# Attention followed by a SwiGLU block: value products one pair later, the first sequence's exponentials summed on the tensor engine, weights rounded by integer operations

## The chip, the cores and the metric

The kernel runs on one NeuronCore of one Trainium2 chip. The metric is the device time of one execution in microseconds (us); the number given for a kernel is the median of several runs.

The engines of the core have queues of their own, each worked off in order: TensorE (PE in the profile, with its weight loads as PEld) does matmuls and transposes, VectorE (DVE), ScalarE (ACT) and GpSimd (POOL) work on tiles, and SyncE (SP) issues DMAs here. They meet at semaphores.

## The reference

Attention with normalised queries and keys, then a feed-forward block over its output, all in float32 (the weights arrive as float64):

```python
batch, n_heads, seq, head_dim = (8, 12, 448, 64)
n_tokens, d_model, d_ff = (3584, 768, 1536)

def rmsnorm(x, g):
    rms = np.sqrt(np.mean(x * x, axis=-1, keepdims=True) + 1e-06)
    return x / rms * g
q_n, k_n = (rmsnorm(q, g_q), rmsnorm(k, g_k))
scores = scale * np.matmul(q_n, k_n.transpose(0, 1, 3, 2))
attn = np.exp(scores - np.max(scores, axis=-1, keepdims=True))
attn = attn / (np.sum(attn, axis=-1, keepdims=True) + 1e-09)
x = np.matmul(attn, v)          # then (B,H,S,D) -> (B*S, H*D)

xn = x / rms(x) * rms_g
g = xn @ w_gate
silu = g * (1.0 / (1.0 + np.exp(-g)))
out = (silu * (xn @ w_val)) @ w_out
```

## The kernel before

There are 8 sequences of 448 tokens, and in each 12 heads that are worked two at a time: 6 pairs a sequence, 48 pairs in all (`g` counts them). `safe_scores` is the part that runs; a second version, `any_scores`, stands behind a flag that is not set for these inputs.

**A pair of heads.** `load_pair` issues five DMAs on SP. `norm_pair` squares q and k on ScalarE (L463), sums rows on VectorE (L466), and on GpSimd scales the sums, raises them to the power -1/2 (L469) and multiplies q by the result (L471). `turn_pair` transposes q and k on TensorE (L485) and copies them to SBUF, the query by ScalarE (L488) and the key by VectorE (L490). `score` does four score matmuls (two blocks of 112 keys by two heads, L500), ScalarE's exponentials (L504), and GpSimd's additions (L508 and L512) that sum the exponentials of the four key blocks into one tile `es` for each head: six additions a pair. It is called twice a pair. `values` does the value products (L520) and multiplies `es` by a matrix of ones (L524), which gives the softmax denominators; `divide` takes their reciprocal on VectorE (L532), multiplies (L537), and sums the squares of the result on ScalarE and GpSimd (L542, L543).

**The feed-forward.** When six pairs of a sequence are done, `rms_x` and `norm_x` normalise their output. `ffn_items` lists 24 projections of six matmuls (`gate` and `val`, L575) and six to eight output projections of 12 matmuls (L600). `fill`, which is called four times a pair, emits such items of the sequence before between the attention steps of the present one, by their cost in columns. So the first sequence's attention runs with no feed-forward beside it, and the last sequence's feed-forward runs alone. The projections write to two PSUM banks (`ps_f`), which VectorE empties (L584 and L590, behind ScalarE's tanh, L582).

**Weights.** `convert` turns a block of 128 x 768 float64 weights into float32 by its two 32-bit words: ScalarE's absolute value of the high word (L413), GpSimd's clip (L414), VectorE's shift and sign (L416, L417), then the power of two of the value (L420), the low word times that power (L422), and GpSimd's float addition (L423). There are 36 blocks: 12 of the gate, 12 of the value projection, which are also stored to DRAM for the later sequences, and 12 of the output projection. Three gate and three value blocks are converted during the first sequence's attention; the other 30 when the first sequence's feed-forward runs, each three projections ahead of its use. The float64 blocks come into two buffers (`raw_pool`).

**What sets the order.** The program lists the work pair by pair; a scheduler then orders each engine's instructions, so an engine's row of instructions can differ from the listing. A buffer's next use waits for its last reader.

## Time and profile before

| | us |
|---|---|
| median of 3 runs | 1904.11 (1902.02 to 1904.52) |
| the profiled execution | 1902.34 |
| its span, first to last instruction | 1900.4 |
| TensorE busy | 1788.5 (94%) |
| GpSimd busy | 687.4 (36%) |
| VectorE busy | 577.8 (30%) |
| ScalarE busy | 412.7 (22%) |
| DMA, mean over the span | 78 GB/s |

The shares are means over stages that differ. The stages are seen in the granted TensorE clock and in the busy time by stretch: the first sequence's attention (to about 154 us), then the first sequence's feed-forward beside the second one's attention (its gate and value projections until 369 us), then six more sequences in the same way, and a feed-forward alone at the end. Matmuls overlap one another in the profile, so the time that a group takes is read from its start to the start of the next group. Each float32 matmul of the program is two MATMUL records in the trace.

### The profile page before, as it was taken

How to read it: one execution, taken by the hardware profiler on the slowest of the kernel's cores; microseconds unless marked ns; L12 is line 12 of the kernel's file. 1: busy time of each engine (PE TensorE's matmuls, PEld its weight loads, DVE VectorE, ACT ScalarE, POOL GpSimd, SP SyncE). 2: the span in 40 equal slices, each digit the busy share in tenths (PEclk: the TensorE clock that was granted, in tenths of full speed). 3: DMA queues.
4: the chain of work that ended last, by engine and by line, in shares of the span. 5: the costliest groups of instructions: out<-in, count | busy, mean ns of one | idle time of the engine just before them, and what ended most of it. 6: DMA issues, size and time to landing. Idle time of an engine off the chain costs nothing. (4 is left out here: it accounts for less than half of the span.)

```text
span 1900.4 us, 15809 instructions
## 1 busy us (share of the span) xinstructions
PE 1788.5 (94%) x5888; PEld 880.5 (46%) x5888; DVE 577.8 (30%) x618; ACT 412.7 (22%) x689; POOL 687.4 (36%) x563
## 2 busy tenths in 40 slices
PE   4768777899999999999999999999999999999998
PEld 2224333354445544454445544454445544455554
DVE  5445767622221232322221222222231223211100
ACT  3331222312222122212212122212222122210000
POOL 6875666623333233322333233332433233220000
PEclk9788888999999999999999999999999999999999
DMA  4422545312321132312321132312231122202200
GB/s 141 138 68 98 163 148 171 124 34 79 100 78 46 40 90 81 87 32 78 90 82 40 48 91 78 93 35 73 79 90 48 40 84 84 67 26 67 83 17 27
DMA packets 154474, 148.99 MB, mean 78 GB/s; under 512 B 95509, under 2 KB 124693, under 8 KB 154389
## 3 DMA queue, kind: packets, MB, share of 16 engines
q1 hardware_dynamic: 153280, 147.88, 26.3%
q8 instruction: 49, 0.80, 0.2%
q14 instruction: 37, 0.29, 0.1%
q10 hardware_dynamic: 1108, 0.00, 0.0%
HBM read 127.41 MB, written 20.45 MB: 78 GB/s over the span
## 5 line engine op out<-in xcount | busy, mean ns | idle before, releaser
L575 PE MATMUL ff<-xT,wg 128*128 128x448 f32 x1152 | 462.3, 552 | 18.0 <-DVE ga L584 9.8
L575 PE MATMUL ff<-xT,wv 128*128 128x448 f32 x1152 | 463.3, 553 | 15.3 <-DVE hT L590 15.3
L600 PE MATMUL ff<-wo,hT 128*128 128x384 f32 x1344 | 444.9, 489 | 0.0
L600 PEld LDWEIGHTS ff<-wo,hT 128*128 128x128 f32 x1344 | 251.5, 190 | 182.6 <-issue 17.6
L575 PEld LDWEIGHTS ff<-xT,wg 128*128 128x128 f32 x1152 | 217.9, 193 | 245.3 <-issue 233.6
L575 PEld LDWEIGHTS ff<-xT,wv 128*128 128x128 f32 x1152 | 216.9, 193 | 244.8 <-issue 218.6
L512 POOL TENSOR_TENSOR es<-es,e 112x448 f32<-112x448 f32 x192 | 223.3, 1190 | 153.4 <-ACT e L504 153.3
L504 ACT ACTIVATE e<-sc,rs 112x448 f32<-112x448 f32 x384 | 212.4, 635 | 210.4 <-PE sc L500 210.4
L508 POOL TENSOR_TENSOR es<-e 112x448 f32<-112x448 f32 x96 | 109.8, 1163 | 266.0 <-ACT e L504 266.0
L500 PE MATMUL sc<-qkT 64*112 64x448 f32 x768 | 184.7, 578 | 9.4 <-ACT e L504 8.5
L520 PE MATMUL av<-e,vt 112*64 112x448 f32 x768 | 165.8, 577 | 10.0 <-ACT qkT L488 6.1
L584 DVE SCALAR_TENSOR_TENSOR ga<-th,ff 128x448 f32<-128x448 f32 x96 | 59.5, 620 | 379.6 <-ACT th L582 379.6
L532 DVE RECIPROCAL rd<-den 128x448 f32<-128x448 f32 x48 | 141.9, 2955 | 107.1 <-PE den L524 107.1
L590 DVE SCALAR_TENSOR_TENSOR hT<-ga,ff 128x448 f32<-128x448 f32 x96 | 59.5, 620 | 322.5 <-PE ff L575 322.5
L582 ACT ACTIVATE th<-ff 128x448 f32<-128x448 f32 x96 | 52.0, 542 | 411.7 <-PE ff L575 411.7
L469 POOL TENSOR_TENSOR rs<-ms,mhalf 112x16 f32<-112x16 f32 x48 | 139.7, 2910 | 3.9
L500 PEld LDWEIGHTS sc<-qkT 64*112 64x112 f32 x768 | 68.2, 178 | 118.3 <-issue 90.2
L520 PEld LDWEIGHTS av<-e,vt 112*64 112x64 f32 x768 | 53.5, 144 | 111.8 <-issue 98.1
L543 POOL TENSOR_TENSOR ss<-ss,s 128x448 f32<-128x448 f32 x40 | 45.5, 1139 | 144.4 <-ACT s L542 144.4
L467 POOL TENSOR_SCALAR ms<-ms 112x16 f32<-112x16 f32 x48 | 10.6, 220 | 229.0 <-DVE ms L466 228.2
L471 POOL TENSOR_TENSOR qn<-qk,rs 112x512 f32<-112x512 f32 x48 | 50.7, 1057 | 96.8 <-PE tr L485 96.4
L608 DVE COPY y<-ff 128x384 f32<-128x384 f32 x28 | 15.6, 557 | 224.0 <-PE ff L600 209.1
(45 smaller groups left out, 783.1 us busy)
## 6 DMA issues: line engine op xcount, KB each, us to landing
wg<-kept_g SPq DMA_DIRECT2D x84, 384.0 KB, 3.0
wv<-kept_v SPq DMA_DIRECT2D x84, 384.0 KB, 3.0
qk<-in_q_dram SPq DMA_DIRECT2D x96, 112.0 KB, 3.1
qk<-in_k_dram SPq DMA_DIRECT2D x96, 112.0 KB, 2.8
vt<-in_v_dram SPq DMA_DIRECT2D x48, 224.0 KB, 2.6
raw<-in_moe_w_gate_dram SPq DMA_DIRECT2D x12, 768.0 KB, 4.3
raw<-in_moe_w_val_dram SPq DMA_DIRECT2D x12, 768.0 KB, 4.7
raw<-in_moe_w_out_dram SPq DMA_DIRECT2D x12, 768.0 KB, 4.4
```

What stands on the lines that cost most here:

```text
L469: nc.gpsimd.tensor_tensor(rs, ms, mhalf[0:P, :], ALU.pow)
L500: nc.tensor.matmul(ps, lhsT=qkT[r, 1, c * P:(c + 1) * P], rhs=qkT[r, 0, :], start=True, stop=True)
L504: nc.scalar.activation(e, ps, ACT.Exp, scale=rs[:, n:n + 1])
L508: nc.gpsimd.tensor_tensor(es, st["e", g, 0, j], st["e", g, 1, j], ALU.add)
L512: nc.gpsimd.tensor_tensor(es, es, st["e", g, c, j], ALU.add)
L520: nc.tensor.matmul(av[j * D:(j + 1) * D, 0:S], lhsT=vt[:, j, c, :], rhs=st["e", g, c, j], start=(c == 0), stop=(c == NT - 1))
L532: nc.vector.reciprocal(rd, den[:, 0:S])
L575: nc.tensor.matmul(ps, lhsT=wt[:, c, :], rhs=st["xT", b][:, c, :], start=(c == 0), stop=(c == NDC - 1))
L582: nc.scalar.activation(th, g, ACT.Tanh, scale=0.5)
L584: nc.vector.scalar_tensor_tensor(ga, th, 1.0, g, ALU.add, ALU.mult)
L590: nc.vector.scalar_tensor_tensor(hT[:, fc, c0:c0 + S], st.pop(("ga", b, fc)), 0.5, st.pop(("v", b, fc)), ALU.mult, ALU.mult)
L600: nc.tensor.matmul(ps, lhsT=hT[:, fc, i * 128:(i + 1) * 128], rhs=wo[:, fc, n * HALF:(n + 1) * HALF], start=(fc == 0), stop=(fc == NFC - 1))
```

## The change

Three things are changed.

The exponentials of the first six pairs are no longer added on GpSimd: `score` returns before the additions, and `values` multiplies each of the eight tiles of exponentials by the matrix of ones and lets the sums build up in PSUM, in a bank of `ps_f`. From the second sequence on the additions stay.

`values` and `divide` of pair g now stand in a function `finish`, which is called in the round of pair g+1, between the query and the key transposes of pair g+2. `turn_pair` is cut into `turn(g, 0)` for the query and `turn(g, 1)` for the key; loads and normalisations run one pair further ahead. Buffers grow accordingly (`c_qk` and `c_raw` from 2 to 3, `c_e` from 10 to 13, `es` from 3 to 4).

`convert` replaces the power, the multiplication and the float addition. ScalarE turns the low word into an integer of units of the last place, in the input's buffer, and GpSimd adds it to the high part as integers. Six of the twelve output-projection blocks are converted during the first sequence's attention, two blocks a pair, and the other six at every second projection later.

```diff
-    qk_pool, v_pool, qn_pool, qkT_pool = pool("c_qk", 2), pool("c_v", 3), pool("c_qn", 1), pool("c_qkT", 2)
-    e_pool, tmp, y_pool = pool("c_e", 10), pool("c_tmp", 8), pool("c_y", 2)
+    qk_pool, v_pool, qn_pool, qkT_pool = pool("c_qk", 3), pool("c_v", 3), pool("c_qn", 1), pool("c_qkT", 2)
+    e_pool, tmp, y_pool = pool("c_e", 13), pool("c_tmp", 8), pool("c_y", 2)
...
-        power = cv_pool.tile([128, DM], I32, name="power")
-        nc.vector.tensor_scalar(power, top, -(2**23), None, ALU.bitwise_and)
-        low = cv_pool.tile([128, DM], F32, name="low")
-        nc.vector.scalar_tensor_tensor(low, lo.bitcast(U32), 2.0**-52, power.bitcast(F32), ALU.mult, ALU.mult)
-        nc.gpsimd.tensor_tensor(dst.rearrange("p a n -> p (a n)"), top.bitcast(F32), low, ALU.add)
+        nc.scalar.activation(lo, lo.bitcast(U32), ACT.Copy, scale=2.0**-29)
+        nc.gpsimd.tensor_tensor(dst.rearrange("p a n -> p (a n)").bitcast(I32), top, lo, ALU.add)
...
             nc.scalar.activation(e, ps, ACT.Exp, scale=rs[:, n:n + 1])
+        if g < NPAIR:
+            return
...
-        den = st["den", g] = ps_m.tile([128, 512], F32, name="den", tag="m")
-        for j in range(2):
-            nc.tensor.matmul(den[j * D:(j + 1) * D, 0:S], lhsT=ones[0:P, :], rhs=st["es", g, j], start=True, stop=True)
+        den = st["den", g] = (ps_f if g < NPAIR else ps_m).tile([128, 512], F32, name="den", tag="ff" if g < NPAIR else "m")
+
+        terms = [[st["e", g, c, j] for j in range(2)] for c in range(NT)] if g < NPAIR else [[st["es", g, j] for j in range(2)]]
+        for i, pair in enumerate(terms):
+            for j, term in enumerate(pair):
+                nc.tensor.matmul(den[j * D:(j + 1) * D, 0:S], lhsT=ones[0:P, :], rhs=term,
+                                 start=(i == 0), stop=(i == len(terms) - 1))
...
-        if b == 0:
-            weight_out(fc)
+        if b == 0 and fc % 2 == 0:
+            weight_out(NFC // 2 + fc // 2)
...
+    for g in range(NG):
+        b, hp = divmod(g, NPAIR)
+        load_pair(g + 3)
+        score(g, (0, 1))
+        norm_pair(g + 2)
+        fill()
+        turn(g + 1, 0)
+        fill()
+        if g:
+            finish(g - 1)
+        turn(g + 1, 1)
+        score(g, (2, 3))
+        fill()
+        if b == 0:
+            for i in (2 * hp, 2 * hp + 1):
+                if i < 2 * W_AHEAD:
+                    weight("gv"[i % 2], i // 2)
+                else:
+                    weight_out(i - 2 * W_AHEAD)
+    finish(NG - 1)
     fill(len(todo))
```

What this makes of the engines' instructions is seen in three places. TensorE, a middle pair of the first sequence before (`tr` are transposes, `sc` scores, `av` value products, `den` denominators):

```order
L485 MATMUL tr<-ident,qn 128x112 x4
L485 MATMUL tr<-ident,qk 128x112 x4
L520 MATMUL av<-e,vt 64x448 x8
L524 MATMUL den<-es,ones 64x448 x2
L500 MATMUL sc<-qkT 112x448 x8
```

The same engine and place now:

```order
L482 MATMUL tr<-ident,qn 128x112 x4
L519 MATMUL av<-e,vt 64x448 x8
L526 MATMUL den<-e,ones 64x448 x7
L482 MATMUL tr<-ident,qk 128x112 x4
L497 MATMUL sc<-qkT 112x448 x4
L526 MATMUL den<-e,ones 64x448
L497 MATMUL sc<-qkT 112x448 x4
```

The denominators are eight in place of two, one of them drawn ahead between two score groups; the value products are those of a pair earlier, and the key transposes stand behind them.

VectorE, around a reciprocal of the first sequence before (`ms` is the row sum, `qkT` the key copy, `top`, `power` and `low` belong to a weight block):

```order
L490 COPY qkT<-tr 128x448
L416 TENSOR_SCALAR top<-top 128x768
L417 SCALAR_TENSOR_TENSOR top<-raw,top 128x768
L420 TENSOR_SCALAR power<-top 128x768
L422 SCALAR_TENSOR_TENSOR low<-raw,power 128x768
L532 RECIPROCAL rd<-den 128x448
L466 TENSOR_REDUCE ms<-sq 112x16
L537 TENSOR_TENSOR xT<-av,rd 128x448
```

And now:

```order
L463 TENSOR_REDUCE ms<-sq 112x16
L416 TENSOR_SCALAR top<-top 128x768
L417 SCALAR_TENSOR_TENSOR top<-raw,top 128x768
L535 RECIPROCAL rd<-den 128x448
L487 COPY qkT<-tr 128x448
L540 TENSOR_TENSOR xT<-av,rd 128x448
```

Two operations a block are gone; the key copy has moved from ahead of the block to behind the reciprocal, and the row sum to ahead of both.

GpSimd, a middle pair of the first sequence before (`rs` is the power, `ss` the sum of squares):

```order
L508 TENSOR_TENSOR es<-e 112x448 x2
L467 TENSOR_SCALAR ms<-ms 112x16
L469 TENSOR_TENSOR rs<-ms,mhalf 112x16
L512 TENSOR_TENSOR es<-es,e 112x448
L414 TENSOR_SCALAR top<-top 128x768
L543 TENSOR_TENSOR ss<-ss,s_518 128x448
L512 TENSOR_TENSOR es<-es,e 112x448
L471 TENSOR_TENSOR qn<-qk,rs 112x512
L512 TENSOR_TENSOR es<-es,e 112x448 x2
L414 TENSOR_SCALAR top<-top 128x768
```

And now:

```order
L468 TENSOR_TENSOR qn<-qk,rs 112x512
L464 TENSOR_SCALAR ms<-ms 112x16
L466 TENSOR_TENSOR rs<-ms,mhalf 112x16
L414 TENSOR_SCALAR top<-top 128x768
L420 TENSOR_TENSOR wo<-top,raw 128x768
L414 TENSOR_SCALAR top<-top 128x768 x2
L546 TENSOR_TENSOR ss<-ss,s_549 128x448
L420 TENSOR_TENSOR wo<-top,raw 128x768 x2
```

The additions of exponentials are gone and weight blocks stand in their place; the clip whose result VectorE needs ahead of the reciprocal stands directly behind the power.

## Rows read from the trace of the kernel before

**Rows 1.** Busy us (instructions) by stretch and engine, granted clock, DMA share, GB/s

```profile
0.00:153.60 153.60, 93.22 (x308) 37.90 (x309) 73.36 (x69) 54.88 (x87) 114.03 (x95) 0.80 0.37 107
153.60:368.70 215.10, 170.31 (x488) 76.98 (x488) 158.72 (x159) 58.13 (x86) 136.21 (x98) 0.87 0.48 155
368.70:1900.40 1531.70, 1524.99 (x5094) 765.66 (x5092) 345.74 (x392) 299.74 (x516) 437.17 (x371) 1.00 0.22 65
```

**Rows 2.** Timeline of TensorE at the boundaries: start, duration, instructions [idle before, releaser]

```profile
15.86 6.34 PE L500 MATMUL sc<-qkT 64*112 64x448 f32 x16 [0.81 <-DVE qkT L490]
...
135.32 5.13 PE L500 MATMUL sc<-qkT 64*112 64x448 f32 x16
...
153.60 6.70 PE L575 MATMUL ff<-xT,wg 128*128 128x448 f32 x12
...
368.71 8.01 PE L600 MATMUL ff<-wo,hT 128*128 128x384 f32 x24
```

**Rows 3.** Timeline of TensorE in a stretch without idle time

```profile
730.21 0.55 PE L485 MATMUL tr<-ident,qk 112*128 112x112 f32 x4
730.59 4.69 PE L575 MATMUL ff<-xT,wv 128*128 128x448 f32 x12
735.21 3.23 PE L520 MATMUL av<-e,vt 112*64 112x448 f32 x16
738.26 0.92 PE L524 MATMUL den<-es,ones 112*64 112x448 f32 x4
739.12 4.78 PE L575 MATMUL ff<-xT,wg 128*128 128x448 f32 x12
743.82 1.76 PE L500 MATMUL sc<-qkT 64*112 64x448 f32 x8
```

**Rows 4.** Instructions by line, 0 to 368.7 us: busy us, mean ns | idle before, releaser

```profile
L512 POOL TENSOR_TENSOR es<-es,e 112x448 f32<-112x448 f32 x44 | 60.6, 1391 | 0.1
L504 ACT ACTIVATE e<-sc,rs 112x448 f32<-112x448 f32 x88 | 49.4, 635 | 39.6 <-PE sc L500 39.6
L417 DVE SCALAR_TENSOR_TENSOR top<-raw,top 128x768 int32<-128x768 int32 x36 | 48.2, 1340 | 0.9
L422 DVE SCALAR_TENSOR_TENSOR low<-raw,power 128x768 f32<-128x768 uint32 x36 | 42.2, 1172 | 0.9
L416 DVE TENSOR_SCALAR top<-top 128x768 int32<-128x768 int32 x36 | 39.8, 1107 | 85.1 <-POOL top L414 85.0
L469 POOL TENSOR_TENSOR rs<-ms,mhalf 112x16 f32<-112x16 f32 x13 | 37.8, 2910 | 1.0
L413 ACT ACTIVATE top<-raw 128x768 f32<-128x768 f32 x36 | 32.9, 915 | 137.1 <-DMA raw<-in_moe_w_val_dram 46.1 <-DMA raw<-in_moe_w_out_dram 36.9 <-DMA raw<-in_moe_w_gate_dram 31.7
L420 DVE TENSOR_SCALAR power<-top 128x768 int32<-128x768 int32 x36 | 31.3, 870 | 1.0
L532 DVE RECIPROCAL rd<-den 128x448 f32<-128x448 f32 x10 | 29.5, 2951 | 18.1 <-PE den L524 18.1
L423 POOL TENSOR_TENSOR wo<-top,low 128x768 f32<-128x768 f32 x12 | 22.2, 1849 | 20.8 <-DVE low L422 20.8
L466 DVE TENSOR_REDUCE ms<-sq 112x16 f32<-112x1024 f32 x14 | 16.7, 1195 | 3.8 <-ACT sq L463 3.8
L463 ACT ACTIVATE sq<-qk 112x1024 f32<-112x1024 f32 x14 | 14.8, 1058 | 25.4 <-DMA qk<-in_k_dram 25.4
L490 DVE COPY qkT<-tr 128x448 f32<-128x448 f32 x12 | 7.4, 614 | 3.8 <-PE tr L485 3.8
```

**Rows 5.** Timeline of the engines around one stall of TensorE

```profile
197.52 0.83 POOL L414 TENSOR_SCALAR top<-top 128x768 f32<-128x768 f32 x1
...
198.38 2.15 DVE L416 TENSOR_SCALAR top<-top 128x768 int32<-128x768 int32 x1 [3.30 <-POOL top L414]
...
203.03 0.61 DVE L590 SCALAR_TENSOR_TENSOR hT<-ga,ff 128x448 f32<-128x448 f32 x1
...
203.79 2.58 PE L575 MATMUL ff<-xT,wv 128*128 128x448 f32 x3 [5.71 <-DVE hT L590]
```

More of the change, by code (lines that the diff above doesn't have):

```diff
@@ L355, in safe_scores @@
     const, small = pool("c_const", 1), pool("c_small", 4)
-    qk_pool, v_pool, qn_pool, qkT_pool = pool("c_qk", 2), pool("c_v", 3), pool("c_qn", 1), pool("c_qkT", 2)
-    e_pool, tmp, y_pool = pool("c_e", 10), pool("c_tmp", 8), pool("c_y", 2)
+    qk_pool, v_pool, qn_pool, qkT_pool = pool("c_qk", 3), pool("c_v", 3), pool("c_qn", 1), pool("c_qkT", 2)
+    e_pool, tmp, y_pool = pool("c_e", 13), pool("c_tmp", 8), pool("c_y", 2)
     xT_pool, w_pool = pool("c_xT", 2), pool("c_w", 3)
-    raw_pool, cv_pool = pool("c_raw", 2), pool("c_cv", 2)
+    raw_pool, cv_pool = pool("c_raw", 3), pool("c_cv", 2)
     scratch = pool("c_dram", 1, space=DRAM)
@@ L473, in norm_pair, with turn @@
             rs[:, 0:2 * NT].unsqueeze(2).to_broadcast([P, 2 * NT, D]), ALU.mult)
-    def turn_pair(g):
+    def turn(g, i):
         if g >= NG:
             return
-        qk, qn = st.pop(("qk", g)), st.pop(("qn", g))
-        qkT = st["qkT", g] = qkT_pool.tile([128, 2, S], F32, name="qkT")
-        for i in range(2):
-            ps = ps_m.tile([128, NT, P], F32, name="tr", tag="m")
-            for t in range(NT):
-                src = (qn if i == 0 else qk[:, 1])[:, t * 2 * D:(t + 1) * 2 * D]
-                nc.tensor.transpose(ps[:, t, :], src, ident[0:P, 0:P])
-            flat = ps.rearrange("p t n -> p (t n)")
-            if i == 0:
-                nc.scalar.activation(qkT[:, i, :], flat, ACT.Copy, scale=gqk[:, 0:1])
-            else:
-                nc.vector.tensor_copy(qkT[:, i, :], flat)
+        if i == 0:
+            src, st["qkT", g] = st.pop(("qn", g)), qkT_pool.tile([128, 2, S], F32, name="qkT")
+        else:
+            src = st.pop(("qk", g))[:, 1]
+        ps = ps_m.tile([128, NT, P], F32, name="tr", tag="m")
+        for t in range(NT):
+            nc.tensor.transpose(ps[:, t, :], src[:, t * 2 * D:(t + 1) * 2 * D], ident[0:P, 0:P])
+        dst, flat = st["qkT", g][:, i, :], ps.rearrange("p t n -> p (t n)")
+        if i == 0:
+            nc.scalar.activation(dst, flat, ACT.Copy, scale=gqk[:, 0:1])
+        else:
+            nc.vector.tensor_copy(dst, flat)
     def score(g, cs):
@@ L504, in score @@
             nc.scalar.activation(e, ps, ACT.Exp, scale=rs[:, n:n + 1])
+        if g < NPAIR:
+            return
         for j in range(2):
             if cs[0] == 0:
-                es = st["es", g, j] = tmp.tile([P, S], F32, name="es", tag="es", bufs=3)
+                es = st["es", g, j] = tmp.tile([P, S], F32, name="es", tag="es", bufs=4)
                 nc.gpsimd.tensor_tensor(es, st["e", g, 0, j], st["e", g, 1, j], ALU.add)
@@ L644, in fill, with finish @@
                 n -= 1
-    load_pair(0)
-    load_pair(1)
-    norm_pair(0)
-    turn_pair(0)
-    for g in range(NG):
-        b, hp = divmod(g, NPAIR)
-        load_pair(g + 2)
-        norm_pair(g + 1)
-        score(g, (0, 1))
-        if b == 0 and hp < W_AHEAD:
-            weight("g", hp)
-        fill()
-        score(g, (2, 3))
-        if b == 0 and hp < W_AHEAD:
-            weight("v", hp)
-        fill()
-        turn_pair(g + 1)
-        fill()
+    def finish(g):
+        nonlocal todo, total, spent, slot
+        b, hp = divmod(g, NPAIR)
         values(g)
@@ L675, in safe_scores @@
             total, spent, slot = sum(c for c, _ in todo[:-LEFT]), 0.0, 0
+    for g in range(3):
+        load_pair(g)
+    norm_pair(0)
+    turn(0, 0)
+    turn(0, 1)
+    norm_pair(1)
+    for g in range(NG):
[15 more added lines that the diff above has]
+                    weight("gv"[i % 2], i // 2)
+                else:
+                    weight_out(i - 2 * W_AHEAD)
+    finish(NG - 1)
     fill(len(todo))
```

## The prediction

> **What bounds the kernel now.** I read the busy time and granted clock by stretch first [rows 1]. From 368.7 us to the end TensorE has work for 1525.0 of 1531.7 us at a granted clock of 1.00: there the time is the sum of its matmuls, and only added or removed matmuls, or a lost cover, count. All that can be won lies before. Up to 153.6 us, where the first feed-forward matmul starts [rows 2], TensorE is busy 93.2 us and its mean clock is 0.80, that is partly at 1.2 GHz; GpSimd (POOL) is busy 114.0 us. From 153.6 to 368.7 us TensorE is busy 170.3 of 215.1 us at 0.87.
>
> Then the boundaries [rows 2]: scores of the first pair at 15.86 us, of the seventh pair (first of the second sequence) at 135.32, six steps of 19.9 us; 18.3 us later the feed-forward begins.
>
> Then the costs [rows 4] and one stall [rows 5]. The summing of exponentials on GpSimd takes 1.39 us an addition, six a pair, 8.3 us. A weight block costs ScalarE 0.92, VectorE 1.11 + 1.34 + 0.87 + 1.17 = 4.49, and GpSimd 0.83 for the clip and 1.85 for the last addition. In the stall the clip comes late (197.52), VectorE, which is in order, stands at the shift that needs it (198.38, stretched to 2.15 us beside GpSimd's addition), the gating product hT behind it ends at 203.64, and TensorE, whose two output banks are full, starts 0.15 us later after 5.71 us idle. In this stretch the one pattern of stall is: TensorE waits for VectorE, which waits for GpSimd.
>
> **First stretch: sums on TensorE, values one pair later.** Removed: six pairs of additions on GpSimd, 6 x 8.3 = 50 us of its 114. Added to TensorE: eight denominator matmuls a pair in place of two. Two take 0.86 us from start to start (738.26 to 739.12) [rows 3], so eight take 3.4, and six pairs pay 6 x 2.6 = 15 us of TensorE. A pair is then two score groups 3.5, two transposes 0.8, values 3.05 and denominators 3.4, 10.8 us at full clock, below the step of 19.9: it lies beside other work unless the clock stays low.
>
> What sets the step now? The order shows a loop through five engines: the scores of pair g+1 need the copy of its transposed keys, which stands on VectorE behind the reciprocal of pair g-1, this behind a weight block's two bit operations, these behind the clip on GpSimd, and this behind the power that normalises pair g+2, whose squares stand on ScalarE behind the exponentials of pair g. Its length by [rows 4], with the clip and the hand-overs by [rows 5]: first exponential 0.9 us after the scores start (half of 1.76 [rows 3]), four exponentials at 49.4/88, 2.25, the new ScalarE conversion 0.92 (the nearest row is the Abs over the same 768 strided words; bounds 0.56 and 1.06, ScalarE's rows at 448 and 1024 elements), query copy 0.6 (as the key copy), squares 1.06, row sum 1.20, power 2.91, clip 0.83, shift and sign 2.45, reciprocal 2.95, key copy 0.61, and nine hand-overs of 0.03 to 0.15, about 0.7: 17.4. With the two VectorE operations less stretched it is under 17; I take 17. The first step has no reciprocal in it: 7 us (scores, exponentials, squares of a pair that is loaded meanwhile). One of the other five has its clip ahead of the power, 3 us less. The seventh pair's scores then start at 15.9 + 7 + 5 x 17 - 3 = 105 us.
>
> From there the last pair of the sequence has to be finished, which the delay puts behind the seventh pair's first scores: 1.8 + 0.4 + 3.05 + 3.4 = 8.6 us on TensorE. Then reciprocal, product, square, GpSimd's sum of squares, the small power and the scaling. Before, from the last denominators' end to the first gate matmul, these take the 18.3 us of [rows 2], with an earlier power and late additions in GpSimd's queue. I keep 12.4 of them, since one power and about two additions (2.91 + 2 x 1.39) are no longer in front; all 18.3 or only 9 are the bounds. Feed-forward starts at 105 + 8.6 + 12.4 = 126 us: a **gain of 27.6** (153.6 - 126). Bounds: steps at TensorE's 10.8 us give about 105; steps at 19.9 with the longer tail about 145.
>
> **Second stretch: weight blocks.** Six of the 30 blocks move into the first stretch, where they are in the loop above already, and each of the 24 left loses 0.87 + 1.17 on VectorE and gains 0.92 on ScalarE, whose 58 us of 215 [rows 1] hide it. Three input buffers in place of two take the load off the loop. TensorE's own work here, from start-to-start lengths [rows 3]: 24 groups x 4.70 = 112.8, nine score halves x 1.76 = 15.8, five pairs of values and denominators x 3.91 = 19.6, ten transposes x 0.38 = 3.8: 152 us, so 63 of the 215.1 are lost. One block after the other, clip, VectorE's operations and the addition take 0.83 + 4.49 + 1.85 = 7.17 us, and 30 of them 215 us, the whole stretch; after, 0.83 + 2.45 + 1.85 = 5.13, and 24 take 123, less than TensorE's 152. So the blocks cease to set the pace, but GpSimd has 24 x 2.68 = 64 us for them and 5 x 13.7 = 68 for the pairs (additions 8.3, power 2.9, and two further operations for which I take 2.5, a little under two additions): 132 of 152. In-order queues at 87% will still run into each other; I leave a fifth of the loss, 13 us: 165 us, a **gain of 50**. Bounds: 152, and 195 as in the third case below.
>
> The integer addition that ends a block is in no row. Its nearest are 1.85 us (float, two inputs of the same size) and, either way, 0.83 (one input) and 2.91 (the power, the slowest operation GpSimd runs here). I take 1.85.
>
> The Trainium skill ("GPSIMD Engine Reference", section "Performance pitfalls for Q7 kernels") says that GpSimd pays half as much again per element once a read steps by more than 8 bytes. The new addition reads every second 4-byte word, exactly 8 bytes, so by that rule it pays nothing; no row of before has such a read on GpSimd. If it paid, the addition would be 2.8 us and the time that of the third case.
>
> **From 368.7 us on.** Exponentials are still added on GpSimd and no matmul is added. Splitting the two transposes changes the order of groups: a score group lasts 1.76 where eight matmuls at the values' pace of 3.05/16 would be 1.53, so a changed neighbour costs up to 0.2 us; 42 pairs, 0 to 8 us. I take **3 lost**. The one-pair delay adds no wait in the shown order: a feed-forward group of 4.70 stands, but for once a sequence, between the key transposes' score group and the next scores, more than the reciprocal's 2.95. Value loads and squares issue one pair earlier on SP, with a third buffer, past weight loads that have one more buffer as well: nothing is exposed. The final feed-forward is unchanged.
>
> **Sum.** 27.6 + 50 - 3 = 74.6. The profiled execution took 1902.34 (span 1900.4), so 1827.7; the median of the runs is 1904.11, 1.8 above: **1829**.
>
> **The rivals.** (1) Forecast, 1829; with its own terms' bounds, 1808 to 1850. Chance 0.60. (2) The loop breaks because VectorE is seldom stretched and TensorE alone paces both stretches: 105 and 152 us, gains of 48.6 and 63, nothing lost later: 1904.1 - 112 = 1792. For it: GpSimd loses half of its load in the first stretch. Against it: the loop stands in the order. 0.15. (3) GpSimd becomes the bound of the second stretch, because its addition takes 2.91: 24 x 3.74 + 68 = 158 us, which at the share of 81% that the forecast gives it (132 of 165) is 195; the first stretch gets 5 us longer: gains of 22.6 and 20, less 3: 1864. 0.10. (4) The first stretch does not shorten, so the moved sums don't do what they say. TensorE's clock stays at 1.2 GHz there, as the mean of 0.80 [rows 1] allows; a pair is then 21.6 us of matmuls, the scores of the seventh pair start at 15.9 + 7 + 108 = 131, the feed-forward near 153: only 50 - 3 remain: 1857. Against it: the clock is mostly granted while pauses are short, and the order keeps TensorE busy 11 of 17 us. 0.09. (5) Slower: the cover in the later sequences is lost. Scores of the next pair wait there for the key copy behind the reciprocal; 2.95 us in each of 42 pairs are 124: 1953. It decides from 74.6 / 42, some 1.8 us a pair, on. Against it: TensorE has no idle time there [rows 1] and the group in between is longer. 0.04. Left over, 0.02 for no change.
>
> The Trainium skill ("TensorE: Matmul & The Clock Gate", section "Part 1: The HAM clock gate") calls the throttled clock the default, which activity releases. By that rule sums on TensorE help themselves to the clock and (4) is unlikely; the trace agrees in that it grants 1.00 where TensorE is always busy.
>
> **How the numbers follow.** About 0.2% (3.8 us) is what a measurement can tell from no change. Cases 1 to 4 are faster: 0.94; same 0.02; slower 0.04. The range takes the forecast with its bounds and most of cases 2, 3 and 4: 1790 to 1866.
>
> **What would show it.** Right: the first gate matmul near 126 us (105 to 145), scores of successive first-sequence pairs some 17 us apart with VectorE's reciprocal directly behind a block's sign operation; no additions of exponentials on GpSimd before the seventh pair; the first output-projection matmul near 126 + 165 = 291 us; from there to the end 1532 to 1540 us at clock 1.00. Wrong: an integer addition over 2.4 us, idle TensorE after 300 us, or steps of 20 us.

## The result and the profile after

The changed kernel takes 1849.3 us (median; 1849.24 to 1850.28) against 1903.9 of the kernel before in the same comparison: a ratio of 0.9716, 95% interval 0.9699 to 0.9733. The prediction was 1829, range 1790 to 1866: direction and range hold, the gain is 54.6 us where 74.6 was forecast. The profiled execution has a span of 1848.4 us, 52.0 less than before.

Line numbers have moved by a few: in the changed kernel L463 is the row sum, L466 the power, L482 the transposes, L487 the key copy, L497 the scores, L501 the exponentials, L526 the denominators, L535 the reciprocal, L578 the gate and value projections, L603 the output projections; L414, L416 and L417 still are a block's clip, shift and sign, L419 is the new ScalarE conversion and L420 the new integer addition.

The three stretches of [rows 1], cut at the same two events (columns as there):

```profile
0.00:138.15 138.15, 95.35 (x384) 39.31 (x384) 66.05 (x66) 73.96 (x110) 90.48 (x74) 0.87 0.51 151
138.15:318.90 180.75, 160.04 (x497) 73.05 (x497) 104.54 (x91) 72.23 (x105) 120.81 (x90) 0.93 0.52 162
318.90:1848.40 1529.50, 1522.77 (x5082) 768.07 (x5080) 340.05 (x390) 295.62 (x510) 426.85 (x363) 1.00 0.23 65
```

The first stretch is 15.45 us shorter (153.60 to 138.15; forecast 27.6), the second 34.35 (215.10 to 180.75; forecast 50), the rest 2.2 shorter (forecast 3 longer). In the rest nothing has changed but the cut: it holds 12 TensorE records fewer, a score group and its transposes that now stand ahead of it.

TensorE at the boundaries, as in [rows 2] (the first scores of the first, second, third, fourth and seventh pair, the first gate matmul, the first output projection):

```profile
16.18 3.12 PE L497 MATMUL sc<-qkT 64*112 64x448 f32 x8 [0.81 <-DVE qkT L487]
...
24.61 4.18 PE L497 MATMUL sc<-qkT 64*112 64x448 f32 x8 [2.69 <-ACT e L501]
...
47.30 3.33 PE L497 MATMUL sc<-qkT 64*112 64x448 f32 x8 [6.09 <-DVE qkT L487]
...
63.75 3.23 PE L497 MATMUL sc<-qkT 64*112 64x448 f32 x8 [2.88 <-DVE qkT L487]
...
116.12 1.76 PE L497 MATMUL sc<-qkT 64*112 64x448 f32 x8 [0.50 <-DVE qkT L487]
...
138.15 6.59 PE L578 MATMUL ff<-xT,wg 128*128 128x448 f32 x12
318.90 8.01 PE L603 MATMUL ff<-wo,hT 128*128 128x384 f32 x24
```

The steps are 8.4, 22.7, 16.4, 18.0, 18.0 and 16.4 us (the fifth and sixth pair start at 81.73 and 99.76), the tail from 116.12 to the gate matmul 22.0. The waits of TensorE (waits, engine and line waited for: us in total, times, longest) are few and have new names:

```profile
PE sc L497 <- DVE qkT L487: 15.2, 5, 6.1
...
PE tr L482 <- DVE rd L535: 10.1, 2, 7.6
PE ff L578 <- DVE ga L587: 7.2, 4, 3.8
PE sc L497 <- ACT e L501: 6.6, 2, 3.9
...
PE ff L578 <- DVE hT L593: 3.4, 2, 2.1
```

Left out are the start-up (13.6 us, as before) and the waits of the tail. Scores that wait for the key copy are the loop of the prediction, and lie in the first stretch, as do the two waits for exponentials (the first and the fifth step); key transposes that wait for the reciprocal (10.1 us), and projections that wait for VectorE (7.2 + 3.4), are the second stretch. The costs of the new and the stretched operations, 0 to 318.9 us, as in [rows 4]:

```profile
L416 DVE TENSOR_SCALAR top<-top 128x768 int32<-128x768 int32 x36 | 49.4, 1373 | 77.9 <-POOL top L414 77.9
...
L419 ACT ACTIVATE raw<-raw 128x768 int32<-128x768 uint32 x36 | 33.3, 924 | 15.9 <-DMA raw<-in_moe_w_out_dram 7.4 <-DMA raw<-in_moe_w_gate_dram 6.6 <-DMA raw<-in_moe_w_val_dram 1.9
...
L420 POOL TENSOR_TENSOR wv<-top,raw 128x768 int32<-128x768 int32 x12 | 23.1, 1928 | 4.2 <-PE sc L497 2.7 <-issue 1.5
...
L420 POOL TENSOR_TENSOR wo<-top,raw 128x768 int32<-128x768 int32 x12 | 22.4, 1869 | 10.4 <-issue 3.6 <-DVE top L417 3.2 <-ACT qkT L485 1.9
```

The integer addition takes 1.87 to 1.93 us and the conversion 0.92, as forecast. VectorE's shift (L416) has become slower, 1373 ns a block where it was 1107, and all the idle time ahead of it, 77.9 us, is for the clip on GpSimd.

### The profile page after: what moved, and what is told of

Same layout as the page of the kernel before. It is cut to its first block, busy times and chain, and to the rows that moved or that the text cites. A ratio compares the mean times of both kernels' runs of the same rounds, so it can differ in the third digit from the quotient of the medians.

```text
span 1848.4 us, 15816 instructions
## 1 busy us (share of the span) xinstructions
PE 1778.2 (96%) x5960; PEld 880.4 (48%) x5960; DVE 510.6 (28%) x546; ACT 441.8 (24%) x725; POOL 638.1 (35%) x527
## 3 DMA queue, kind: packets, MB, share of 16 engines
q1 hardware_dynamic: 153280, 147.88, 27.6%
## 5 line engine op out<-in xcount | busy, mean ns | idle before, releaser
L578 PE MATMUL ff<-xT,wg 128*128 128x448 f32 x1152 | 457.0, 547 | 7.3 <-DVE ga L587 7.2
L578 PE MATMUL ff<-xT,wv 128*128 128x448 f32 x1152 | 456.6, 546 | 3.4 <-DVE hT L593 3.4
L603 PE MATMUL ff<-wo,hT 128*128 128x384 f32 x1344 | 444.6, 488 | 0.0
L603 PEld LDWEIGHTS ff<-wo,hT 128*128 128x128 f32 x1344 | 251.6, 190 | 182.2 <-issue 14.9
L578 PEld LDWEIGHTS ff<-xT,wg 128*128 128x128 f32 x1152 | 215.7, 191 | 231.6 <-issue 212.0
L578 PEld LDWEIGHTS ff<-xT,wv 128*128 128x128 f32 x1152 | 214.3, 191 | 229.6 <-issue 215.3
L511 POOL TENSOR_TENSOR es<-es,e 112x448 f32<-112x448 f32 x168 | 187.0, 1145 | 289.3 <-ACT e L501 289.3
L501 ACT ACTIVATE e<-sc,rs 112x448 f32<-112x448 f32 x384 | 214.2, 636 | 160.8 <-PE sc L497 160.7
L497 PE MATMUL sc<-qkT 64*112 64x448 f32 x768 | 185.4, 590 | 21.8 <-DVE qkT L487 15.2
L535 DVE RECIPROCAL rd<-den 128x448 f32<-128x448 f32 x48 | 141.9, 2956 | 180.6 <-PE den L526 180.6
L519 PE MATMUL av<-e,vt 112*64 112x448 f32 x768 | 159.1, 557 | 0.0
L466 POOL TENSOR_TENSOR rs<-ms,mhalf 112x16 f32<-112x16 f32 x48 | 140.4, 2926 | 4.0
L463 DVE TENSOR_REDUCE ms<-sq 112x16 f32<-112x1024 f32 x48 | 58.5, 1219 | 216.8 <-ACT sq L460 201.2
L497 PEld LDWEIGHTS sc<-qkT 64*112 64x112 f32 x768 | 66.7, 180 | 104.4 <-issue 58.0
L507 POOL TENSOR_TENSOR es<-e 112x448 f32<-112x448 f32 x84 | 94.1, 1140 | 50.7 <-ACT e L501 50.7
L545 ACT ACTIVATE s<-xT 128x448 f32<-128x448 f32 x40 | 23.1, 577 | 327.7 <-DVE xT L540 327.7
```

Source lines behind the costliest of these rows:

```text
L463: nc.vector.tensor_reduce(out=ms, in_=sq.rearrange("p (n d) -> p n d", d=D), axis=AX_X, op=ALU.add)
L466: nc.gpsimd.tensor_tensor(rs, ms, mhalf[0:P, :], ALU.pow)
L497: nc.tensor.matmul(ps, lhsT=qkT[r, 1, c * P:(c + 1) * P], rhs=qkT[r, 0, :], start=True, stop=True)
L501: nc.scalar.activation(e, ps, ACT.Exp, scale=rs[:, n:n + 1])
L507: nc.gpsimd.tensor_tensor(es, st["e", g, 0, j], st["e", g, 1, j], ALU.add)
L511: nc.gpsimd.tensor_tensor(es, es, st["e", g, c, j], ALU.add)
```

## The experiments

Each kernel is timed beside the kernel before; "after" is the changed kernel. The first gate matmul ends the first stretch, the first output projection the second; these two columns are read from one execution each.

| kernel | median us | against after | first gate | second stretch |
|---|---|---|---|---|
| after | 1849.3 | | 138.15 | 180.75 |
| integer conversion alone, on the kernel before | 1881.0 | | 147.10 | 197.56 |
| sums back on GpSimd | 1870.3 | +21.0 | 158.22 | 181.06 |
| power twice | 1863.5 | +14.2 | 149.88 | 182.43 |
| key transposes ahead of the values | 1858.9 | +9.6 | 146.46 | 183.46 |
| no delay by a pair | 1842.0 | -7.3 | 132.32 | 175.62 |
| clip on VectorE | 1826.2 | -23.1 | 123.30 | 169.25 |
| clip on VectorE, no delay | 1832.1 | -17.2 | 125.88 | 172.36 |
| all twelve output blocks late | 1857.8 | +8.5 | 124.86 | 200.79 |
| second sequence's sums on TensorE | 1845.9 | -3.4 | 133.86 | 178.43 |
| the same and the clip on VectorE | 1827.1 | -22.2 | 122.02 | 172.23 |
| filling behind the values | 1849.8 | +0.5 | 136.75 | 178.46 |
| the same and the clip on VectorE | 1828.9 | -20.4 | 124.95 | 171.59 |

### What the parts are worth

The sums of the first sequence go back to GpSimd, all else stays:

```diff
-        if g < NPAIR:
-            return
...
-        den = st["den", g] = (ps_f if g < NPAIR else ps_m).tile([128, 512], F32, name="den", tag="ff" if g < NPAIR else "m")
+        den = st["den", g] = ps_m.tile([128, 512], F32, name="den", tag="m")
...
-        terms = [[st["e", g, c, j] for j in range(2)] for c in range(NT)] if g < NPAIR else [[st["es", g, j] for j in range(2)]]
+        terms = [[st["es", g, j] for j in range(2)]]
```

> The changed kernel with the first sequence's exponentials added on GpSimd again; the delay, the integer blocks and their places stay. Theory (the sums' removal from GpSimd carries the first stretch): six pairs give GpSimd 6 x 8.3 = 50 us back, and it is busy 90 of 138 us there already, so it becomes the bound: first gate matmul 20 to 35 us later than at 138, time 1870 to 1885. Rival (the one-pair delay and the integer blocks brought it, the sums lay beside other work): first gate matmul within 5 us of 138, time 1845 to 1855.

1870.3 us, ratio to the kernel before 0.9822 (0.9805 to 0.9838). The sums are worth 21 us, 20.1 of them before the first gate matmul and 0.3 behind. What waits there without them is seen in one row of TensorE's waits:

```profile
PE tr L482 <- DVE rd L533: 43.4, 7, 8.7
```

The denominators then take one of the two PSUM banks (`ps_m`) that also serve the transposes and value products, and key transposes wait seven times until the reciprocal gives it back. The changed kernel keeps the first sequence's denominators in a projection bank (`ps_f`). This run puts the additions on GpSimd and the bank back, so it prices them together; no run separates them. The mean granted clock of the first stretch is 0.76 here, 0.87 in the changed kernel.

The integer conversion alone, in the kernel before:

```diff
-        nc.vector.tensor_scalar(power, top, -(2**23), None, ALU.bitwise_and)
...
-        nc.vector.scalar_tensor_tensor(low, lo.bitcast(U32), 2.0**-52, power.bitcast(F32), ALU.mult, ALU.mult)
-        nc.gpsimd.tensor_tensor(dst.rearrange("p a n -> p (a n)"), top.bitcast(F32), low, ALU.add)
+        nc.scalar.activation(lo, lo.bitcast(U32), ACT.Copy, scale=2.0**-29)
+        nc.gpsimd.tensor_tensor(dst.rearrange("p a n -> p (a n)").bitcast(I32), top, lo, ALU.add)
```

> The kernel before with only the integer rounding of weight blocks (two VectorE operations replaced by one on ScalarE). Theory (in the second stretch the blocks' serial path set the pace, 7.17 us against 5.13 a block): the stretch from first gate matmul to first output projection falls from 215 to about 175 to 185, the first stretch by 0 to 6 with its six blocks; time 1865 to 1878. Rival (the stretch shrank because six blocks moved out of it and the input has three buffers): 1890 to 1904.

1881.0 us, ratio 0.9883 (0.9867 to 0.99): 22 us, between the two ranges. 6.5 come off the first stretch and 17.5 off the second, which is 197.6 us and not the 175 to 185 of the theory: the blocks' serial path was at most a part of what set the pace there.

### The loop in the first sequence

The power is computed a second time for pairs three to eight, which changes no value:

```diff
+        if 2 <= g < 8:
+            nc.gpsimd.tensor_tensor(rs, ms, mhalf[0:P, :], ALU.pow)
         nc.gpsimd.tensor_tensor(rs, ms, mhalf[0:P, :], ALU.pow)
```

> The changed kernel with GpSimd's power done twice for pairs 2 to 7 (2.9 us more each, same result). Theory (power, clip, block, reciprocal and key copy are one loop): four of the steps have the power ahead of the clip and get 2.9 longer each, so about 12 us and at most 17: 1859 to 1866. Rival (the steps are paced by TensorE; GpSimd has 48 us idle in 138): 1848 to 1852.

1863.5 us (ratio 0.9788, 0.9771 to 0.9804); the first gate matmul is 11.7 us later, four times the power's 2.91, and the wait of scores for the key copy grows from 15.2 to 27.8 us. The second to the fifth step grow by 4.9, 2.6, 2.9 and 3.0 us; the sixth, whose power is that of the ninth pair and not doubled, stays at 16.4. GpSimd's power is in the path that sets the steps. The changed kernel's trace has the loop in so many rows; timeline of all engines, fourth to fifth pair:

```profile
72.93 2.91 POOL L466 TENSOR_TENSOR rs<-ms,mhalf 112x16 f32<-112x16 f32 x1
...
75.82 0.83 POOL L414 TENSOR_SCALAR top<-top 128x768 f32<-128x768 f32 x1
...
76.68 0.56 DVE L416 TENSOR_SCALAR top<-top 128x768 int32<-128x768 int32 x1 [5.36 <-POOL top L414]
77.28 0.96 DVE L417 SCALAR_TENSOR_TENSOR top<-raw,top 128x768 int32<-128x768 int32 x1
78.15 2.95 DVE L535 RECIPROCAL rd<-den 128x448 f32<-128x448 f32 x1
...
81.02 0.56 DVE L487 COPY qkT<-tr 128x448 f32<-128x448 f32 x1
...
81.73 2.58 PE L497 MATMUL sc<-qkT 64*112 64x448 f32 x6 [4.93 <-DVE qkT L487]
```

The denominators that this reciprocal needs end at 73.7 (the two matmuls at 75.83 are the next pair's, drawn ahead), and the keys are transposed by 74.21. From 76.80 on TensorE idles 4.93 us, because reciprocal and key copy stand behind a weight block that waits for GpSimd.

If the reciprocal is in the loop, the key copy should profit from standing ahead of it:

```diff
-        if g:
-            finish(g - 1)
         turn(g + 1, 1)
+        if g:
+            finish(g - 1)
```

> The changed kernel with the key transposes listed ahead of finish(g - 1), so that the key copy stands ahead of the reciprocal on VectorE. Theory (a loop through the reciprocal, the weight block's operations, clip and power sets the step of the first sequence): without the reciprocal's 2.95 and its wait in it, the last five steps of 16.4 to 22.7 us shrink by 3 to 4 each, 15 to 20 in all; the 10 us in which key transposes waited for the reciprocal in the second stretch go too: 1820 to 1830. Rival (TensorE's own matmuls at a low clock pace the steps): steps as they are, only the 10 us or less are won: 1839 to 1849.

A miss: 1858.9 us, slower (ratio 0.9761, 0.9745 to 0.9778). The reciprocal did leave the path: scores wait 0.8 us for key copies, once. But the seventh pair's scores start near 113 in place of 116, and the first gate matmul comes 33 us after them, not 22. The step has a second chain of nearly the same length, through ScalarE (timeline around the third step):

```profile
68.50 0.63 ACT L485 ACTIVATE qkT<-tr,gqk 128x448 f32<-128x448 f32 x1
...
69.19 3.23 PE L519 MATMUL av<-e,vt 112*64 112x448 f32 x16 [2.05 <-ACT qkT L485]
```

The value products wait for the query copy, which stands on ScalarE behind squares (66.51 to 67.57) and exponentials; scores wait 17.4 us for exponentials (6.6 in the changed kernel). And at the sequence's end GpSimd's sum of squares stands behind a power (134.57) besides the four additions of the next pair (4.39 us at 130.21) that stand there in the changed kernel as well, so the tail grew.

### The delay and the clip

No delay: `finish(g)` in its own round, behind both transposes, with sums and conversion as in the changed kernel.

```diff
-        turn(g + 1, 0)
-        fill()
-        if g:
-            finish(g - 1)
-        turn(g + 1, 1)
         score(g, (2, 3))
         fill()
+        turn(g + 1, 0)
+        turn(g + 1, 1)
+        fill()
+        finish(g)
...
-    finish(NG - 1)
```

> The changed kernel with finish(g) in its own round again, behind both score groups and both transposes; sums on TensorE and integer blocks stay. Theory (the delay takes the exponentials' wait out of a step, and the sums need it since TensorE can't sum before the last exponential): steps of the first sequence 1 to 3 us longer, no tail behind the seventh pair's scores; time 1850 to 1865. Rival (the delay only moved the end of the sequence one round on): 1835 to 1849.

1842.0 us (ratio 0.9678, 0.9662 to 0.9694): 7.3 below the changed kernel, against the theory that I had put first. The delay costs time here, 5.8 us before the first gate matmul and 5.1 in the second stretch. Waits for key copies fall from 15.2 to 0.8 us, those for the reciprocal from 10.1 to none.

Next, the one link in the loop that has no need to be on GpSimd:

```diff
-        nc.gpsimd.tensor_scalar(top.bitcast(F32), top.bitcast(F32), 122879.9921875, 2.0**-15, ALU.min, ALU.max)
+        nc.vector.tensor_scalar(top.bitcast(F32), top.bitcast(F32), 122879.9921875, 2.0**-15, ALU.min, ALU.max)
```

> The changed kernel with the clip of each weight block (L414) on VectorE in place of GpSimd, so that VectorE no longer waits for GpSimd's power and additions ahead of the reciprocal, the key copy and the gating products. Theory (VectorE waiting in order for GpSimd's clip is what sets the first sequence's steps and most stalls of the second stretch): four steps lose about 3 us each, the second stretch comes down from 181 to about 160 to 168; time 1815 to 1832. Rival (other loops of nearly the same length, or VectorE's own load, take over at once): 1838 to 1852.

1826.2 us (1821.4 to 1828.8; ratio 0.9596, 0.9575 to 0.9616): 23 us below the changed kernel and the lowest median of all. Both stretches gain, 14.9 and 11.5 us:

```profile
0.00:123.30 123.30, 89.48 (x384) 37.67 (x384) 76.64 (x80) 72.87 (x110) 82.02 (x60) 0.91 0.59 169
123.30:292.55 169.25, 155.87 (x497) 71.62 (x497) 113.86 (x113) 72.10 (x105) 105.50 (x68) 0.96 0.54 173
```

In the first stretch the second step gives 6.5 us (22.7 to 16.2), the fourth to the sixth 1.5 to 2.5 each, the third nothing. The first step is 1.9 shorter too, but it is 6.5 us also in the run with the power twice, so that is hardly the clip's doing.

VectorE is busy longer than in the changed kernel (114 for 105 us in the second stretch) and yet its work is done sooner: what its queue waited for, not its load, was the cost. The shift (L416) and the sign (L417) in the second stretch of the changed kernel, as in [rows 4]:

```profile
L416 DVE TENSOR_SCALAR top<-top 128x768 int32<-128x768 int32 x22 | 37.5, 1705 | 47.5 <-POOL top L414 47.5
L417 DVE SCALAR_TENSOR_TENSOR top<-raw,top 128x768 int32<-128x768 int32 x22 | 28.7, 1306 | 0.7
```

And with the clip (L414) on VectorE:

```profile
L417 DVE SCALAR_TENSOR_TENSOR top<-raw,top 128x768 int32<-128x768 int32 x22 | 34.1, 1549 | 0.7
L414 DVE TENSOR_SCALAR top<-top 128x768 f32<-128x768 f32 x22 | 24.3, 1105 | 23.9 <-ACT top L413 23.9
L416 DVE TENSOR_SCALAR top<-top 128x768 int32<-128x768 int32 x22 | 17.6, 800 | 0.7
```

VectorE's wait ahead of a block falls from 47.5 us for GpSimd to 23.9 for ScalarE. A second cost stays. On GpSimd the clip that releases the shift has a block's integer addition directly behind it, so shift and addition start together (below, 167.31 and 167.38) and the shift ends 0.4 us after the addition. With the clip on VectorE the shift is mostly free of this, and clip and sign are stretched in its place: against 0.56, 0.56 and 0.96 us for clip, shift and sign alone, the blocks' operations are 30 us too long there (76.0 for 45.8) and 33 in the changed kernel (66.2 for 33.4). As a total, then, the collision hardly changes, and the gain goes with the wait. GpSimd is relieved of the clips as well (busy 105.5 us for 120.8); no run separates that from the wait.

With the clip on VectorE, does the delay still cost? The same edit as above without the delay:

> Edit on the changed kernel: the clip of a weight block on VectorE (as in the run with the clip alone, 1826.2 us, first gate matmul at 123.3, first output projection at 292.6) and, besides, no delay of the values by a pair (as in the run without the delay, 1842.0 us, 7.3 below the changed kernel). Theory A: the delay costs because it sets the reciprocal, behind VectorE's shift that waits for GpSimd's clip, in front of the key copy. With the clip on VectorE this wait is gone already, so removing the delay brings little or harms: the denominators' and the key transposes' hand-overs come back into the same round. 1823 to 1835 us, first gate matmul 121 to 130. Theory B: the delay costs by itself, the reciprocal's 2.95 us in the path of the key copy and the longer tail behind the seventh pair's scores, whatever the clip does. Then its 7 us come off again: 1815 to 1821 us, first gate matmul 115 to 120.

1832.1 us (1828.9 to 1832.7; ratio 0.9626, 0.961 to 0.9642). Removing the delay no longer gains: the median is 6 us higher. That it loses is not clear of noise, since the slowest run with the delay (1828.8) and the fastest without it (1828.9) are only 0.1 us apart and the intervals overlap. But the second theory, 1821 us at most, is out, and the first fits: what the delay costs in the changed kernel is the clip's lateness, which it puts in front of the key copy by way of the reciprocal.

### Where the work stands

All twelve output-projection blocks beside the second sequence, none in the first:

```diff
-        if b == 0 and fc % 2 == 0:
-            weight_out(NFC // 2 + fc // 2)
+        if b == 0:
+            weight_out(fc)
...
-                else:
-                    weight_out(i - 2 * W_AHEAD)
```

> The changed kernel with all twelve output-projection blocks in the second stretch, one at each projection pair, as before. Theory (weight blocks are in the loop of a step): rounds four to six have no block, their steps fall from 16.4 to 18 to about 13 to 15, 8 to 12 us in all; the second stretch gets six blocks more at about 6 us: 30 to 36 longer; time 1868 to 1878. Rival (TensorE paces the second stretch, blocks lie beside it): 1838 to 1850.

1857.8 us (ratio 0.9763, 0.9747 to 0.9779), between the two ranges. The first stretch is 13.3 us shorter, a little more than I allowed, the second 20.0 longer, less than expected: moving six blocks forward is worth 8.5 us. The step from the sixth to the seventh pair, with no block beside it, takes 12.1 us (90.77 to 102.85) in place of 16.4, not far from TensorE's own 10.8.

The second sequence's exponentials summed on TensorE too (both conditions on `g < NPAIR` become `g < 2 * NPAIR`; the denominators stay in `ps_m` there):

> The changed kernel with the second sequence's exponentials summed on TensorE too. TensorE gets about 15 us of matmuls more, GpSimd loses 50 us in and around the second stretch. Theory (GpSimd's queue is what stalls VectorE and so TensorE there): the second stretch shrinks by 5 to 12 us although five of the six pairs' sums, 13 us, are added; time 1838 to 1848. Rival (TensorE's work paces it, the stalls come from VectorE's own operations): the sums add to the time: 1858 to 1866.

1845.9 us (ratio 0.9702, 0.9686 to 0.9719), 3.4 below. In the second stretch TensorE's waits for the gating products fall from 10.6 to 1.3 us, and it is busy 6.9 us more: the stretch shrinks by 2.3, not by the 5 to 12 expected. 4.3 us come off the first stretch, in whose tail the seventh pair's additions are gone too, and the rest is 2.2 longer. The same with the clip on VectorE:

> Edit on the changed kernel: the clip of a weight block on VectorE (alone: 1826.2 us, second stretch 169.3 us) and the exponentials of the second sequence summed on TensorE as well (alone: 3.4 us below the changed kernel, second stretch 178.4 in place of 180.8). Theory A: the second sums help only because they take GpSimd's additions from in front of the clip. With the clip on VectorE nothing on TensorE's path waits for GpSimd in that stretch, and the 36 added matmuls are five to six times 2.6 us on the engine that is now nearly the bound: 1834 to 1842 us, second stretch 178 to 185. Theory B: GpSimd's additions still delay the blocks (its last addition of a block, and the tiles' release), and the two gains add up: 1818 to 1826 us, second stretch 162 to 169.

1827.1 us (ratio 0.9597, 0.9581 to 0.9613), between the two and no better than the clip alone: against that run TensorE is busy 9.9 us more in the second stretch (165.8 for 155.9) and idle 6.9 less.

### The key transposes that wait in the second stretch

The reciprocal's 10.1 us were not in my prediction. One of the two stalls in the changed kernel (timeline):

```profile
163.55 0.92 PE L526 MATMUL den<-es,ones 112*64 112x448 f32 x4
...
165.38 4.78 PE L578 MATMUL ff<-xT,wg 128*128 128x448 f32 x12 [0.91 <-DVE ga L587]
...
167.31 1.83 POOL L420 TENSOR_TENSOR wv<-top,raw 128x768 int32<-128x768 int32 x1
167.38 2.18 DVE L416 TENSOR_SCALAR top<-top 128x768 int32<-128x768 int32 x1 [0.87 <-POOL top L414]
...
171.69 2.17 DVE L416 TENSOR_SCALAR top<-top 128x768 int32<-128x768 int32 x1 [0.60 <-POOL top L414]
...
174.77 2.95 DVE L535 RECIPROCAL rd<-den 128x448 f32<-128x448 f32 x1
...
177.78 1.01 PE L482 MATMUL tr<-ident,qk 112*128 112x112 f32 x4 [7.62 <-DVE rd L535]
```

The denominators are done by 164.5. Two blocks go before the reciprocal on VectorE, with shifts of 2.2 us, and only its end at 177.7 frees the bank into which the keys are transposed. The next test puts more work into that gap:

```diff
-        fill()
         if g:
             finish(g - 1)
+        fill()
         turn(g + 1, 1)
```

> Edit on the changed kernel: in a round, the filling with feed-forward work that stood ahead of the value products now stands behind them, ahead of the key transposes. So two projections of six matmuls, in place of one, stand on TensorE between the denominators and the key transposes of the second sequence, which need the PSUM bank that the reciprocal gives back. In the first sequence there is nothing to fill with, so the first gate matmul stays at 138 us. Theory A: the wait of the key transposes for the reciprocal, 10.1 us in two stalls (7.6 and 2.5), is a matter of place; another 4.7 us of work in front of them takes up to 7.2 of it, and a little more where TensorE's clock had fallen after the stall. Second stretch 171 to 175 us, 1839 to 1844 us. Theory B: VectorE itself is late at this place, and the projections put there wait for VectorE's emptying of their banks; the stall is named otherwise but is as long. Second stretch 178 to 184 us, 1846 to 1853 us.

1849.8 us (ratio 0.9721, 0.9708 to 0.9735), no change. The time is that of the second theory, but the stall is in neither place. From TensorE's waits:

```profile
PE den L526 <- ACT qkT L485: 15.1, 3, 6.6
```

No transpose waits for the reciprocal any more; now the denominators wait, three times, for the query copy, which holds the other bank of `ps_m` and stands on ScalarE behind conversions. Query transposes, values, denominators and key transposes take turns in two banks. With a projection between the first two the copy had its time; moved, that projection covers the one hand-over (a bank passed on when its reader is done) and uncovers the other.

With the clip on VectorE beside it:

> Edit on the changed kernel: the clip of a weight block on VectorE (alone 1826.2 us, second stretch 169.3 us with 7.3 us of key transposes that wait for the reciprocal) and the filling behind the value products, as in the run beside this one. Theory A (place): up to 7 us more come off, second stretch 161 to 165 us, 1818 to 1823 us. Theory B (VectorE is late, and with the clip it has more to do): the stall moves to the projections' banks, second stretch 168 to 173 us, 1825 to 1831 us.

1828.9 us (ratio 0.9609, 0.9596 to 0.9623), again no gain, and the denominators wait 12.5 us for query copies. A third bank wasn't tried: scores take four, these two and the projections two, together the eight that the program has declared.

## Why the prediction was right, and where it was wrong

**The frame held.** The last stretch stands as before, no TensorE wait lies behind 318.9 us, and the gain comes from the two stretches named. So the fifth rival (cover lost in 42 pairs) is out, the fourth (first stretch not shortened) by the 15.45 us, and the third by the integer addition, 1.87 to 1.93 us and not 2.91. The Trainium skill ("GPSIMD Engine Reference", "Performance pitfalls for Q7 kernels") lets a step of exactly 8 bytes go free, and this trace agrees: the float addition before took 1.85 [rows 4]. The second rival (TensorE alone sets the pace, 1792) is reached by no kernel here.

**The loop was right, two of its steps were not.** The forecast had 15.9 us, a first step of 7, five steps of 82 together (17 each, less 3 for one), a tail of 21.0. Measured: 16.2, 8.4, 91.5 and 22.0. The tail and the start-up are right to 1 us. Of the five steps the third, fourth and sixth take 50.8 us together where 51 was summed. Two terms failed: the second step takes 22.7 and not 17, and the fifth, the one whose clip stands ahead of the power, 18.0 and not 14. The second step, all engines:

```profile
31.74 1.10 ACT L460 ACTIVATE sq<-qk 112x1024 f32<-112x1024 f32 x1
...
33.71 1.05 POOL L468 TENSOR_TENSOR qn<-qk,rs 112x512 f32<-112x512 f32 x1
33.78 1.40 DVE L416 TENSOR_SCALAR top<-top 128x768 int32<-128x768 int32 x1 [2.83 <-POOL top L414]
...
36.08 1.21 DVE L463 TENSOR_REDUCE ms<-sq 112x16 f32<-112x1024 f32 x1
36.30 1.84 POOL L420 TENSOR_TENSOR wv<-top,raw 128x768 int32<-128x768 int32 x1 [1.54 <-issue]
...
38.51 2.91 POOL L466 TENSOR_TENSOR rs<-ms,mhalf 112x16 f32<-112x16 f32 x1
...
41.40 0.83 POOL L414 TENSOR_SCALAR top<-top 128x768 f32<-128x768 f32 x1
```

The squares end at 32.84, but a block's shift and sign stand ahead of the row sum on VectorE until 36.1, and that block's addition ahead of the power on GpSimd until 38.1; the clip of one more block (41.40), which the reciprocal waits for, stands behind the power. The step has two blocks in its loop where I summed one. The fifth step:

```profile
90.45 0.85 POOL L414 TENSOR_SCALAR top<-top 128x768 f32<-128x768 f32 x1
...
95.70 0.56 DVE L487 COPY qkT<-tr 128x448 f32<-128x448 f32 x1
...
98.29 0.90 ACT L413 ACTIVATE top<-raw 128x768 f32<-128x768 f32 x1 [5.55 <-POOL wo L420]
99.10 1.66 ACT L501 ACTIVATE e<-sc,rs 112x448 f32<-112x448 f32 x3
...
99.76 4.26 PE L497 MATMUL sc<-qkT 64*112 64x448 f32 x8 [3.86 <-ACT e L501]
```

Its clip (90.45) does come ahead of the power (92.04), and the key copy is done at 96.26, 3.5 us before the scores start. But the block's addition stands behind the power on GpSimd; ScalarE, in order, waits for it 5.55 us at the Abs of a later block, which needs the addition's tile back, and the exponentials that free the scores' bank stand behind this Abs. The power stays in the step by a path that my loop didn't have; with the power twice this step, too, grew by 3.0 us. The two terms make 5.7 + 4.0 of the 12.2 us by which the gate matmul missed 126; the first step (8.4 for 7, and 6.5 in the run with the power twice), the tail and the start are the other 2.5.

**The second stretch: a wait that was left out.** Of 180.75 us TensorE is busy 160.0 and idle 20.7, where 152 + 13 was the sum. The 13 for coupling answers to 10.6 us of waits for gating products: near, though a fifth of the loss was a judgement and not worked out, so that is luck. What was missing is a wait for a bank. For the later sequences I had reasoned that the delay adds none, since a projection stands between the key transposes and the next scores, and there it came out so. In the second stretch the sum has no term for it, but there the bank binds the denominators and the key transposes ahead of that projection: 10.1 us. The kernel before had waits of this sort, between 153.6 and 368.7 us:

```profile
PE den L524 <- DVE qkT L490: 7.9, 2, 7.3
```

Its denominators don't read the key copy; what they wait for is the bank. Where I wrote of one pattern of stall, this was a second. In the first sequence the changed kernel's denominators have a bank elsewhere; in the run that puts bank and sums back, such waits are 43.4 us, 31.8 of them in the first stretch. The other 8 us are busy time beyond the 152, at a mean clock of 0.93. And that 30 blocks of 7.17 us made 215, the whole stretch, proved little: with the conversion alone 30 blocks of 5.13 make 154, and the stretch still took 197.6. The granted clock after three stalls of 3.75, 2.20 and 2.09 us (windows of the projection that follows each, columns as in [rows 1]):

```profile
202.19:208.66 6.47, 6.47 (x14) 2.94 (x16) 5.59 (x5) 1.73 (x2) 4.04 (x4) 0.74 0.93 310
232.46:237.20 4.74, 4.74 (x14) 2.46 (x15) 1.28 (x1) 0.57 (x2) 4.74 (x3) 1.00 0.42 145
239.68:246.15 6.47, 6.47 (x14) 2.97 (x16) 6.30 (x3) 3.99 (x7) 6.04 (x6) 0.74 0.60 187
```

A projection takes 4.7 us at a granted 1.00 and 6.5 at 0.74, where the clock was partly at 1.2 GHz. In the first stretch it goes the other way: the mean clock rises from 0.80 to 0.87, and is 0.76 in the run with the delay and without the sums on TensorE.

**The rest** was to lose up to 8 us by reordered groups: it lost nothing. The 2.2 us are the moved cut; the kernels here with 5094 records behind it take 1531.7 us, as before.

**The parts.** Conversion 22 us (alone), sums 21, the blocks moved forward 8.5, the delay -7.3, each taken by itself: 44 of 54.6. They aren't independent, as the delay shows, which costs 7.3 us with the clip on GpSimd and nothing with the clip on VectorE; what the added input buffers bring was not measured alone. The argument was right about which engines and queues set the pace. It never priced the delay by itself, which the run without it shows to cost, and it followed the loop through VectorE and not through ScalarE and the banks.

## What to carry to other kernels

When an in-order queue sets a loop, ask of each operation in it not how long it is but what it waits for: a 0.83 us clip on the loaded engine (GpSimd) cost 23 us, because VectorE's whole queue, the reciprocal and the key copy stood behind it. When a step is moved, follow its buffers as well as its instructions: the order showed a projection as cover, while the bank was held until the reciprocal's end, and more cover in one place was taken from another. And a change that costs time by itself can cease to cost once the late link in front of it is gone, so it is tested again after every fix.

## What the runs showed of the hardware

VectorE's shift of 128x768 words, one input, takes 0.56 us alone. Started 0.07 us behind a GpSimd addition of 1.83 us it takes 2.18: it ends 0.42 us after the addition (167.31 + 1.83 = 169.14; 167.38 + 2.18 = 169.56), as if most of it began only then. Another shift, started 0.07 us behind a multiplication of 1.05 us (33.71 and 33.78), takes 1.40 and ends the same 0.42 us after it. So it isn't shared speed but a stop. The Trainium skill ("SBUF — State Buffer", "Who interferes with whom") says that VectorE in one of its two-port modes and GpSimd exclude each other for a whole instruction, and which one stops is decided by who issued first; this trace agrees. The prediction summed the shift at its mean of 1.11 us [rows 4] and hoped for less of such stretching; the mean became 1.37, since the clip releases the shift at the moment at which GpSimd goes on to the addition.

TensorE idled 2.20 us before one projection and 2.09 before another; the first ran at a granted 1.00, the second, with one projection in between, at 0.74. So a stall's price isn't its length alone: here 1.7 us came on top (6.47 for 4.74), once and not the other time.
